# A transformer layer on one core: the transfer queue put into the program's order, with GpSimd's stores handed over some slots later

## The chip, the cores and the metric

The kernel runs on one core of a Trainium2 chip. The metric is the device time of one execution in microseconds (us). A core has a matrix engine (TensorE, PE in the profile; its weight loads are PEld), a vector engine (VectorE, DVE), an activation engine (ScalarE, ACT), GpSimd (POOL) and a queue that issues transfers (SyncE, SP; SPq marks its issues and waits). Each works through its own instructions in order and waits on semaphores for the others. Transfers move between HBM, which holds the inputs, the output and the kernel's scratch tensors, and on-chip memory.

## What is computed

```python
xn = layernorm(x)                                   # x: 2048 rows of 512
q, k, v = split(xn @ wqkv)                          # 32 heads of 16
p = softmax(q @ k.T * 16 ** -0.5)                   # per head, 2048 x 2048
a = concat_heads(p @ v) @ wo
m = gelu(xn @ w1 + b1) @ w2 + b2                    # hidden width 1792
out = x + a + m
```

Everything is in float32 at the interface. The kernel splits operands into a high and a low float16 part and adds the products of the parts.

## The kernel before

**Tiling.** Attention runs over 32 blocks, counted t = 0 to 31: 8 groups of 4 heads (`NG`) by 4 blocks of 512 queries (`NQB`). A block has 16 units. One call of `unit` (L582) issues 16 score products for unit u of the first pass (`s_half`, into `pS`; DVE takes the row maximum with L250), 16 transposed score products for unit u - 20 of the second pass (`e_half`, into `pT`; ACT exponentiates with L295), the products with v (`v_half`, into `pV`), and some dense products (`pD`) from a generator: the q and k projections first (`project`), then the two MLP products (`mlp`), then the output projection (`o_proj`).

**The hand-off of the maxima.** The second pass needs the negated row maxima of its block, which sit in two more rows of the q stack `qst`. When block t's first pass is over, `store` in `s_end` (L264) transposes the maxima on PE, DVE writes them to `mhl` (L271, L272), SP stores them to `m_d` (L275, two transfers), waits until they have landed, and loads them into `qst` (L280, four transfers). This stands in the program at the end of unit 16t + 16, and the first `pT` product of the block at the start of unit 16t + 20.

**What else goes through SP.** All transfers go through the one queue. Per block there is a chain for the softmax sums: `den_d<-osb` (L333), `dn<-den_d` (L360), a reciprocal on DVE (L336), `den_d<-dn` (L338), `rb<-den_d` (L342), three GpSimd operations (L346 to L348) and the store `ot_d<-ot` (L353). Head stacks `kst` and `qst` are loaded ahead (L392), MLP weights by `fetch_w1` (`wc<-w_d`, L540). In the projection phase GpSimd splits q and k results into `stg` (two buffers, L498 and L499), stored by L483 and L484, and weights into `wsp` (two buffers, L875 to L877), stored by L912 and L914. In the MLP's second product GpSimd adds to `xa`, stored by L995. At the end `oc<-ot_d` (L1006) and `ac<-acc_d` (L1011) load what the output projection needs; `out_dram<-ac` (L1016) stores the result.

**What sets the order.** `later(n, fn)` puts a piece of the program n slots later (a slot is one unit); `tick` (L226) runs what is due, and `pooled` steps for GpSimd are handed out on a budget of 2500 ns a slot. `flush` (L231), called after the projection phase and after the MLP, runs slots without units until no entry marked `True` (the third argument of `later`) is left. From L926 on, the engines in `ORDERED` keep the order in which the program was written. SP is not among them: a scheduler orders its transfers by its own estimates of when they are ready.

Of the kernel before, what the change touches and what calls it, by code (L numbers as in the profile page):

```python
# [25 lines left out]
NF = F // P  # L26
# [10 lines left out]
LFILL = (8, 16, 12, 12)  # L37
WARM = (14, 3, 2, 2)
FINE = "fine"
ORDERED = {mybir.EngineType.PE, mybir.EngineType.Activation, mybir.EngineType.DVE, mybir.EngineType.Pool}  # L40
GELU_C = 0.7978845608028654
GELU_A = 0.044715
MROW = 1024.0
# [4 lines left out]
def layer_kernel(ctx: ExitStack, tc: tile.TileContext, x, wqkv, wo, w1, b1, w2, b2, out):  # L48
# [110 lines left out]
    def given(engine, ns):  # L159
        backlog[engine] += ns  # L160
# [43 lines left out]
    def later(n, fn, local=False):  # L204
        queue.append((slot[0] + n, fn, local))
# [10 lines left out]
    def pooled(*todo):  # L216
        steps.extend(todo)
# [93 lines left out]
    def v_end(u):  # L311

        t, kt = divmod(u, 16)
        g, qb = divmod(t, NQB)
        for h in range(4):
            del ptiles[u, h]
        if kt < 15:
            return
        pv, k = pv_of.pop(t)
        osb = work.tile([P, QB], F32, name="osb", bufs=2)  # L320
        nc.scalar.activation(osb, pv, AF.Copy)
        given("act", 600)
        free_banks["S"].append(k)
        if t == NG * NQB - 1:
            later(1, lambda: last_one(osb))
            return

        dn = work.tile([64, 32], F32, name="dn", bufs=1)
        rb = work.tile([P, QB], F32, name="rb", bufs=1)

        def sums():
            for h in range(4):
                nc.sync.dma_start(den_d[t, 0, h:h + 1, :], osb[32 * h + DH:32 * h + DH + 1, :])  # L333

        def inverse():
            nc.vector.reciprocal(dn, dn)  # L336
            given("dve", 330)
            later(1, lambda: nc.sync.dma_start(den_d[t, 1].rearrange("h (c q) -> (h c) q", q=32), dn))  # L338

        def spread():  # L340
            for h in range(4):
                nc.sync.dma_start(rb[32 * h:32 * h + 32, :], den_d[t, 1, h:h + 1, :].to_broadcast([32, QB]))  # L342

        def store():
            ot = work.tile([P, 2, QB], F16, name="ot", bufs=2)
            pooled((1280, lambda: nc.gpsimd.tensor_tensor(osb, osb, rb, op=ALU.mult)),  # L346
                   (620, lambda: nc.gpsimd.tensor_scalar(ot[:, 0], osb, 1.0, 0.0, op0=ALU.mult, op1=ALU.add)),
                   (1160, lambda: nc.gpsimd.tensor_tensor(ot[:, 1], osb, ot[:, 0], op=ALU.subtract)),  # L348
                   (0, lambda: later(n, put)))

            def put():
                for h in range(4):
                    nc.sync.dma_start(ot_d[64 * g + DH * h:64 * g + DH * h + DH, :, qb * QB:(qb + 1) * QB],  # L353
                                      ot[32 * h:32 * h + DH])
                ready.add(t)


        n, far = (2, 3) if t < (NG - 1) * NQB else (1, 0)
        later(1, sums)
        later(2, lambda: nc.sync.dma_start(dn, den_d[t, 0].rearrange("h (c q) -> (h c) q", q=32)))  # L360
        later(2 + n + far, inverse)
        later(3 + 2 * n + far, spread)
        later(4 + 3 * n + far, store)
# [110 lines left out]
    def project(m, w, sb, wh, bank, early=False):  # L474

        prods = [lambda c=c, i=i, j=j: (wh[:, w, i, c, :], xt[:, j, c, sb * QB:(sb + 1) * QB])
                 for c in range(NC) for i, j in PAIRS]

        dst = qk_d[w, m * P:(m + 1) * P, :, sb * QB:(sb + 1) * QB]

        def finish(pj):
            def put():
                nc.sync.dma_start(dst[:, w:w + 2, :], stg)  # L483
                nc.sync.dma_start(dst[:, 2 - 2 * w, :], stg[:, 0])  # L484

            stg = ph.tile([P, 2, QB], F16, name="stg", bufs=2)
            given("act", 600)
            if early or (w == 1 and not m):
                nc.scalar.activation(stg[:, 0], pj, AF.Copy)
                nc.vector.tensor_tensor(stg[:, 1], pj, stg[:, 0], op=ALU.subtract)  # L490
            else:
                pf = ph.tile([P, QB], F32, name="pf", bufs=2)
                nc.scalar.activation(pf, pj, AF.Copy)
                if not m:
                    nc.scalar.activation(stg[:, 0], pj, AF.Copy)
                    nc.gpsimd.tensor_tensor(stg[:, 1], pf, stg[:, 0], op=ALU.subtract)
                else:
                    hi = lambda: nc.gpsimd.tensor_scalar(stg[:, 0], pf, 1.0, 0.0, op0=ALU.mult, op1=ALU.add)  # L498
                    lo = lambda: nc.gpsimd.tensor_tensor(stg[:, 1], pf, stg[:, 0], op=ALU.subtract)  # L499
                    later(1, lambda: pooled((620, hi), (1160, lo), (0, lambda: later(1, put, True))), True)  # L500
                    return

            put()

        return Group(prods, bank, finish)
# [31 lines left out]
    def fetch_w1(n):  # L537
        if n < NQB * NF:
            wcs[n] = feed[0].tile([P, 2, NC, P], F16, name="wc", bufs=3)
            nc.sync.dma_start(wcs[n], w1_d[n % NF])  # L540
# [89 lines left out]
    with ExitStack() as st1:  # L630
# [249 lines left out]
        def prepare():  # L880
            yield from ms
            am = work.tile([P, 10], F32, name="am_all")
            nc.vector.tensor_reduce(am[:, 0:7], amx[:, 0:7, :], axis=AX.X, op=ALU.max)
            nc.vector.tensor_reduce(am[:, 7:8], b1_s, axis=AX.X, op=ALU.max, apply_absolute_value=True)
            nc.vector.tensor_reduce(am[:, 8:9], amx[:, 7:14, :], axis=AX.XY, op=ALU.max)
            nc.vector.tensor_reduce(am[:, 9:10], amx[:, 14:16, :], axis=AX.XY, op=ALU.max)
            box = []
            yield
            yield from scales(am, 10, sbank, box)
            inv, fac = box  # L890
            fac1.append(fac)

            nc.vector.reduce_max(gs[:, 0:1], fac[:, 0:8], axis=AX.X)
            nc.vector.tensor_tensor(gs[:, 3:4], fac_v[0][:, 0:1], fac[:, 9:10], op=ALU.mult)
            yield
            nc.vector.reciprocal(gs[:, 1:2], gs[:, 0:1])
            nc.vector.tensor_tensor(gs[:, 2:3], gs[:, 0:1], fac[:, 8:9], op=ALU.mult)
            yield
            nc.vector.tensor_scalar_mul(gs[:, 1:2], gs[:, 1:2], 0.5)
            ended = [True]  # L900
            for n in range(16):
                v = fetch(16 + n)
                while not ended[0]:
                    yield
                ended[0] = False

                def then(wh=None, n=n):
                    ended[0] = True
                    if n < 7:
                        for a in range(2):  # L910
                            for l in range(2):
                                nc.sync.dma_start(w1_d[2 * n + a][:, l], wh[:, l, :, a * P:(a + 1) * P])  # L912
                    elif n < 14:
                        nc.sync.dma_start(w2_d[:, :, 2 * n - 14:2 * n - 12, :], wh)  # L914

                if n >= 14:
                    i = 2 * (n - 14)
                    split_steps(wo_s[:, 0, i:i + 2, :], wo_s[:, 1, i:i + 2, :], v, inv[:, 9:10], then)
                    continue
                wh = ph.tile([P, 2, 4, W] if n < 7 else [P, 2, 2, D], F16, name="wsp", bufs=2)  # L920
                k = n if n < 7 else 8
                split_steps(wh[:, 0], wh[:, 1], v, inv[:, k:k + 1], lambda wh=wh, then=then: then(wh))
            while not ended[0]:
                yield

        ctx.enter_context(tc.manual_schedule(engines=ORDERED))  # L926
        fil, pre, more = rest(), prepare(), True
# [7 lines left out]
    def mlp():  # L935
# [25 lines left out]
        for b in range(NQB):  # L961
            xb = xbs[b]
            g = m2.tile([P, 2, NF, QB], F16, name="g", bufs=1)
            for f in range(NF):
                fetch_w1(b * NF + f + 2)
                wc = wcs[b * NF + f]
                if b == 0 and f >= 3:
                    nc.sync.dma_start(w2_s[:, :, f - 3:NF if f == NF - 1 else f - 2, :],
# [13 lines left out]
            for q in range(4):  # L982
# [7 lines left out]
                def store(yp, xa=xa, t=t):  # L990
                    yt = m2.tile([P, D], F32, name="yt", bufs=2)
                    nc.scalar.activation(yt, yp, AF.Copy, scale=gs[:, 2:3])  # L992
                    given("act", 600)
                    add = lambda: nc.gpsimd.tensor_tensor(xa, xa, yt, op=ALU.add)  # L994
                    put = lambda: nc.sync.dma_start(acc_d[t * P:(t + 1) * P, :], xa)  # L995
                    later(1, lambda: pooled((1280, add), (0, lambda: later(1, put, True))), True)

                yield Group([lambda f=f, i=i, j=j, q=q, g=g: (g[:, i, f, q * P:(q + 1) * P], w2_s[:, j, f, :])
                             for f in range(NF) for i, j in PAIRS], dbank, store,
                            lambda n, b=b: (b, n // 3) in done, pace=SLOW if b < 2 else MEAN)  # L1000
# [125 lines left out]
```

## Time and profile before

| | |
|---|---|
| three runs | median 1655.86 us, 1652.38 to 1661.11 |
| the profiled execution | 1654.47 us |
| its span, first to last instruction | 1652.7 us |

The times of rows below are of that one execution and count from the start of its span. This part of its page gives the span in 40 slices of 41.3 us; each digit is a busy share in tenths, PEclk the granted clock of PE, DMA the share of the transfer engines:

```profile
PE   8998889988989999989999999899998999999998
DVE  8887769987988999989898999889898998999921
ACT  4317779987978998979898999888897898999993
POOL 3113577536762111767311167651115764111000
DMA  6466475341121111212111111221111110103122
```

PE, DVE and ACT are all near full from slice 8 on; GpSimd and the transfer engines are not. The projection phase fills slices 3 to 8, the MLP the slices to about 36, the output projection the rest.

### The profile page before, as it was taken

The numbers are of one execution on the slowest core, as the hardware profiler recorded it, in microseconds if no ns is written. First come the engines' busy times: TensorE is split into PE (matmuls) and PEld (weight loads), VectorE is DVE, ScalarE is ACT, GpSimd is POOL, SyncE is SP. The second block draws the span as 40 slices with busy tenths as digits, with TensorE's granted clock in tenths as the row PEclk, the third lists the DMA queues.
The fourth block names the chain that finished last, engine by engine and source line by source line (L and its number), as shares of the span: only waits on it lengthen the run. The fifth ranks groups of instructions, "written<-read, shape, count | busy, mean of one in ns | idle before, by whom it ended". The sixth has DMA issues, their size and how long they took to land.

```text
span 1652.7 us, 85954 instructions
## 1 busy us (share of the span) xinstructions
PE 1545.0 (93%) x38915; PEld 820.7 (50%) x38915; DVE 1427.7 (86%) x2420; ACT 1371.7 (83%) x2254; POOL 652.4 (39%) x678
## 2 busy tenths in 40 slices
PE   8998889988989999989999999899998999999998
PEld 3434445544544555545555555455554454554543
DVE  8887769987988999989898999889898998999921
ACT  4317779987978998979898999888897898999993
POOL 3113577536762111767311167651115764111000
PEclk9999999999999999999999999999999999999999
DMA  6466475341121111212111111221111110103122
GB/s 202 147 196 222 132 197 178 94 150 37 45 62 46 31 32 41 59 36 55 42 43 51 32 42 40 56 59 32 39 43 52 37 32 13 34 26 116 56 89 97
DMA packets 120248, 123.71 MB, mean 75 GB/s; under 512 B 38988, under 2 KB 90572, under 8 KB 119880
## 3 DMA queue, kind: packets, MB, share of 16 engines
q1 hardware_dynamic: 119880, 118.21, 24.4%
q8 instruction: 304, 4.98, 1.3%
q14 instruction: 64, 0.52, 0.1%
HBM read 80.61 MB, written 37.34 MB: 71 GB/s over the span
## 4 chain that ended last, share of the span: by engine, by line
PE 66%; DVE 20%; DMA 5%; issue 3%; POOL 3%; SPq 2%; ACT 1%; DVEq 0%; POOLq 0%
PE pV L169 20%; DVE mt L250 15%; PE pD L169 15%; PE pS L169 14%; PE pT L169 13%; DMA m_d<-mhl 3%; DVE hh L976 2%; DMA qst<-m_d 2%; PE pD L426 1%; PE pT L426 1%; DVE amx L648 1%; PE pT L519 1%; SPq L353 0%; POOL osb L346 0%; POOL ot L348 0%
## 5 line engine op out<-in xcount | busy, mean ns | idle before, releaser
L295 ACT ACTIVATE pe<-pT,sexp 128x512 f32<-128x512 f32 x2048 | 1270.1, 689 | 168.0 <-PE pT L169 110.8
L250 DVE TENSOR_REDUCE mt<-pS 128x1 f32<-128x512 f32 x2048 | 1290.9, 683 | 133.4 <-PE pS L169 112.4
L169 PE MATMUL pV<-pe,vv 64*32 64x512 f32 x8192 | 1098.4, 606 | 1.1 <-PE pS L169 0.7
L169 PE MATMUL pT<-qst,kst 64*32 64x512 f16 x8192 | 710.1, 385 | 67.4 <-DMA qst<-m_d 64.3
L169 PE MATMUL pS<-kst,qst 62*32 62x512 f16 x8192 | 657.6, 385 | 20.6 <-DVE mt L250 14.6
L169 PEld LDWEIGHTS <-kst 64*32 64x32 f16 x8192 | 291.8, 91 | 252.5 <-DMA qst<-m_d 79.6
L169 PEld LDWEIGHTS <-qst 62*32 62x32 f16 x8192 | 280.2, 93 | 263.5 <-issue 131.2
L169 PE MATMUL pD<-w_s,g 64*32 64x512 f16 x5376 | 370.9, 381 | 2.1 <-issue 2.1
L169 PE MATMUL pD<-xb,wc 64*32 64x512 f16 x5376 | 369.5, 384 | 0.6 <-issue 0.6
L169 PEld LDWEIGHTS pV<-pe,vv 64*32 64x32 f32 x8192 | 187.9, 106 | 102.5 <-PE pS L169 7.6
L169 PEld LDWEIGHTS <-wc 64*32 64x32 f16 x5376 | 123.5, 93 | 53.2 <-issue 4.3
L994 POOL TENSOR_TENSOR xa<-xa,yt 128x512 f32<-128x512 f32 x16 | 20.4, 1277 | 322.2 <-ACT yt L992 322.2
L169 PEld LDWEIGHTS <-g 64*32 64x32 f16 x5376 | 114.3, 92 | 46.8 <-issue 4.1
L956 POOL TENSOR_TENSOR t<-hh 128x512 f32<-128x512 f32 x56 | 58.2, 1039 | 196.0 <-DVE hh L976 182.1
L169 PE MATMUL pD<-xt,wqk_h 64*32 64x512 f16 x1920 | 131.6, 387 | 4.0 <-issue 4.0
L346 POOL TENSOR_TENSOR osb<-osb,rb 128x512 f32<-128x512 f32 x31 | 39.8, 1285 | 208.8 <-DMA rb<-den_d 118.2
L958 POOL TENSOR_TENSOR t<-t,hh 128x512 f32<-128x512 f32 x56 | 71.6, 1279 | 4.7
L951 POOL TENSOR_TENSOR t<-t,hh 128x512 f32<-128x512 f32 x56 | 71.5, 1276 | 4.7
L953 POOL TENSOR_TENSOR g<-t,g 128x512 f16<-128x512 f32 x56 | 65.1, 1162 | 4.7
L169 PEld LDWEIGHTS <-wqk_h 64*32 64x32 f16 x1920 | 44.8, 94 | 23.3 <-issue 8.9
L169 PE MATMUL pD<-wo_s,oc 64*32 64x512 f16 x768 | 50.1, 378 | 0.0
L950 POOL TENSOR_SCALAR t<-t,gs 128x512 f32<-128x512 f32 x56 | 38.8, 693 | 24.0 <-ACT t L945 24.0
(137 smaller groups left out, 824.9 us busy)
## 6 DMA issues: line engine op xcount, KB each, us to landing
wch<-in_B_w_dram SPq DMA_DIRECT2D x28, 512.0 KB
wc<-w_d SPq DMA_DIRECT2D x56, 256.0 KB
qk_d<-stg SPq DMA_DIRECT2D x32, 256.0 KB
rb<-den_d SPq DMA_DIRECT2D x124, 64.0 KB
kst<-qk_d SPq DMA_DIRECT2D x128, 48.0 KB
qst<-qk_d SPq DMA_DIRECT2D x128, 48.0 KB
xs<-in_A_x_dram SPq DMA_DIRECT2D x16, 256.0 KB
qk_d<-stg SPq DMA_DIRECT2D x32, 128.0 KB
```

Of the source, the lines that this page charges most:

```text
L169: p = nc.tensor.matmul(*args, **kw)
L250: nc.vector.reduce_max(mt_of[t][:, n, qt, kb:kb + 1], s, axis=AX.X)
L295: nc.scalar.activation(pe, st, AF.Exp, scale=sexp[:, g // 2:g // 2 + 1])
L346: pooled((1280, lambda: nc.gpsimd.tensor_tensor(osb, osb, rb, op=ALU.mult)), (620, lambda: nc.gpsimd.tensor_scalar(ot[:, 0], osb, 1.0, 0.0 ...
L426: nc.tensor.matmul(self.bank, lhs, rhs, start=start, stop=self.last and self.over())
L950: pooled((690, lambda: nc.gpsimd.tensor_scalar(t1, t1, 1.0, gs[:, 1:2], op0=ALU.add, op1=ALU.mult)), (1280, lambda: nc.gpsimd.tensor_tenso ...
L951: (1280, lambda: nc.gpsimd.tensor_tensor(t1, t1, hh, op=ALU.mult)),
L953: (1160, lambda: nc.gpsimd.tensor_tensor(g[:, 1, f, :], t1, g[:, 0, f, :], op=ALU.subtract)),
L956: pooled((1040, lambda: nc.gpsimd.tensor_tensor(t1, hh, hh, op=ALU.mult)), (620, lambda: nc.gpsimd.tensor_scalar(t1, t1, 1.0, 1.0 / GELU_A ...
L958: (1280, lambda: nc.gpsimd.tensor_tensor(t1, t1, hh, op=ALU.mult)),
L976: nc.vector.tensor_scalar(hh, hp, scale, bias, op0=ALU.mult, op1=ALU.add)
L994: add = lambda: nc.gpsimd.tensor_tensor(xa, xa, yt, op=ALU.add)
```

## The change

`ORDERED` gets SP, so that transfers stand in the order in which the program issues them. Stores of what GpSimd made are issued more slots later: `ot_d` 6 slots instead of 2 (still 1 in the last four blocks), `stg` 3 instead of 1, `wsp` 3 instead of at once, `xa` 4 instead of 1. `fetch_w1` inside the MLP is issued one slot later.

```diff
-ORDERED = {mybir.EngineType.PE, mybir.EngineType.Activation, mybir.EngineType.DVE, mybir.EngineType.Pool}
+ORDERED = {mybir.EngineType.SP, mybir.EngineType.PE, mybir.EngineType.Activation, mybir.EngineType.DVE, mybir.EngineType.Pool}
...
-                   (0, lambda: later(n, put)))
+                   (0, lambda: later(1 if n == 1 else 6, put)))
...
-                    later(1, lambda: pooled((620, hi), (1160, lo), (0, lambda: later(1, put, True))), True)
+                    later(1, lambda: pooled((620, hi), (1160, lo), (0, lambda: later(3, put, True))), True)
...
                     ended[0] = True
+                    later(3, lambda: put(wh, n), True)
+
+                def put(wh, n):
                     if n < 7:
...
-                fetch_w1(b * NF + f + 2)
+                later(1, lambda n=b * NF + f + 2: fetch_w1(n))
...
-                    later(1, lambda: pooled((1280, add), (0, lambda: later(1, put, True))), True)
+                    later(1, lambda: pooled((1280, add), (0, lambda: later(4, put, True))), True)
```

**SP around the hand-off of block 12** (the row `m_d<-mhl` is L275 of that block; `x4` counts equal transfers in a row). Before:

```order
L338 DMA den_d<-dn 64x32
L342 DMA rb<-den_d 32x512 x4
L540 DMA wc<-w_d 128x1024
L392 DMA kst_0_2_83<-qk_d 48x512 x2
L392 DMA kst_1_2_87<-qk_d 48x512 x2
L353 DMA ot_d<-ot 32x1x512 x4
L275 DMA m_d<-mhl 32x1x64 x2
L280 DMA qst_0_0_105<-m_d 2x4x128 x2
L280 DMA qst_1_0_109<-m_d 2x4x128 x2
```

With the change:

```order
L353 DMA ot_d<-ot 32x1x512 x4
L540 DMA wc<-w_d 128x1024 x2
L338 DMA den_d<-dn 64x32
L342 DMA rb<-den_d 32x512 x4
L540 DMA wc<-w_d 128x1024
L275 DMA m_d<-mhl 32x1x64 x2
L280 DMA qst_0_0_105<-m_d 2x4x128 x2
L280 DMA qst_1_0_109<-m_d 2x4x128 x2
L540 DMA wc<-w_d 128x1024
L333 DMA den_d<-osb 1x512 x4
```

The store of GpSimd's `ot` no longer stands between `rb` and the hand-off; the one that now stands further ahead is the previous block's. In all blocks but 30 and 31 what stands directly ahead of L275 is of this kind: loads, or stores whose data was made some slots ago.

**SP at the start of the ordered part** (the hand-off of block 0, and the loads of group 1's stacks, `kst_..._89` and following). Before, the 32 stack loads, of which the last two rows are shown, stand ahead of the hand-off:

```order
L392 DMA qst_0_3_108<-qk_d 48x512 x2
L484 DMA qk_d<-stg 128x512
L483 DMA qk_d<-stg 128x2x512
L392 DMA qst_1_3_112<-qk_d 48x512 x2
L275 DMA m_d<-mhl 32x1x64 x2
```

With the change they stand behind it:

```order
L275 DMA m_d<-mhl 32x1x64 x2
L280 DMA qst_0_0_97<-m_d 2x4x128 x2
L280 DMA qst_1_0_101<-m_d 2x4x128 x2
L392 DMA kst_0_0_89<-qk_d 48x512 x2
L392 DMA kst_1_0_93<-qk_d 48x512 x2
L392 DMA kst_0_1_90<-qk_d 48x512 x2
```

The first `stg` stores (L483, L484) now come after 20 of the 32 stack loads and two weight chunks.

**SP and DVE at the end.** On SP, ahead of the last hand-off (block 31), with the change:

```order
L353 DMA ot_d<-ot 32x1x512 x4
L1009 DMA oc<-ot_d 128x2x512 x4
L1014 DMA ac<-acc_d 128x512 x4
L1009 DMA oc<-ot_d 128x2x512 x3
L1009 DMA oc<-ot_d 64x2x512
L1014 DMA ac<-acc_d 128x512 x4
L275 DMA m_d<-mhl 32x1x64 x2
```

Before, six of these sixteen loads stood between `ot_d` and the hand-off, the other ten further ahead. On DVE the reciprocal of block 28 (L336) moves, because the second `flush` now runs more slots (L250 are the row maxima of blocks 29 and 30, `ac` is the output projection's). Before:

```order
L272 SCALAR_TENSOR_TENSOR mhl<-pS,mhl 64x64
L250 TENSOR_REDUCE mt<-pS 128x1 x28
L336 RECIPROCAL dn<-dn 64x32
L250 TENSOR_REDUCE mt<-pS 128x1 x32
L261 TENSOR_REDUCE mneg_118<-mt 128x16
```

With the change:

```order
L272 SCALAR_TENSOR_TENSOR mhl<-pS,mhl 64x64
L250 TENSOR_REDUCE mt<-pS 128x1 x20
L336 RECIPROCAL dn<-dn 64x32
L250 TENSOR_REDUCE mt<-pS 128x1 x40
L1018 SCALAR_TENSOR_TENSOR ac<-pD,gs,ac 128x512
```

It stands 8 reductions, two units, earlier; the output projection's products start three units earlier. Apart from this end, the order on PE, DVE, ACT and GpSimd is the same.

## The prediction

> **What bounds the kernel now.** I read the waits first, then the windows, then the timeline of one block.
>
> ```profile
> PE 1545.0 (93%) x38915; PEld 820.7 (50%) x38915; DVE 1427.7 (86%) x2420; ACT 1371.7 (83%) x2254; POOL 652.4 (39%) x678
> PE pT L169 <- DMA qst<-m_d: 64.3, 21, 6.1
> PE pS L169 <- DVE mt L250: 14.6, 46, 1.7
> DVE mt L250 <- PE pS L169: 112.4, 82, 6.4
> ACT pe L295 <- PE pT L169: 110.8, 89, 7.3
> ```
>
> PE is idle 1652.7 - 1545.0 = 107.7 us. In the waits (total, times, longest), 64.3 us of that is one thing: the first `pT` product of a block waits for the maxima loaded from `m_d`, 21 times. DVE and ACT wait for PE, not the reverse. So the hand-off through SP bounds those moments. Next, what SP itself waited for at the head of its queue:
>
> ```profile
> SPq L353 <- POOL ot L348: 176.8, 29, 10.9
> SPq L540 <- PE pT L169: 149.7, 36, 10.9
> ```
>
> Such waits hold up whatever stands behind them. Block 12 shows it in time order (start, us, engine; the bracket is idle time and its releaser):
>
> ```profile
> 703.89 0.22 DVE L272 SCALAR_TENSOR_TENSOR mhl<-pS,mhl 64x64 f16<-64x64 f32 x1
> 707.97 1.16 POOL L348 TENSOR_TENSOR ot<-osb,ot 128x512 f16<-128x512 f32 x1
> 709.15 2.49 SPq L353 DMA_DIRECT2D ot_d<-ot  x4
> 711.74 2.34 SPq L275 DMA_DIRECT2D m_d<-mhl  x2
> 715.30 1.16 SPq L280 DMA_DIRECT2D qst<-m_d  x4
> 717.17 0.64 PE L169 MATMUL pT<-qst,kst 64*32 64x512 f16 x8 [5.07 <-DMA qst<-m_d]
> ```
>
> `mhl` is ready at 704.11, but SP stands at L353 until GpSimd ends at 709.13, then issues four stores for 2.5 us. The hand-off starts 7.6 us late and PE waits 5.07 us. PE needed the rows at 717.17 - 5.07 = 712.10, 8.0 us after `mhl`. In block 13 no such store is in the way:
>
> ```profile
> 755.19 0.22 DVE L272 SCALAR_TENSOR_TENSOR mhl<-pS,mhl 64x64 f16<-64x64 f32 x1
> 755.43 1.22 SPq L275 DMA_DIRECT2D m_d<-mhl  x2
> 758.98 1.16 SPq L280 DMA_DIRECT2D qst<-m_d  x4
> ```
>
> The last issue ends at 760.14; with the 717.17 - 716.46 = 0.7 us that block 12 needed from there, the rows are in 5.4 us after `mhl`. That is 2.6 us inside the 8.0, and PE does not wait.
>
> The wait is not all. The windows (stretch, length, busy time by engine, PEclk, transfers) show what follows it:
>
> ```profile
> 173.60:1408.50 1234.90, 1152.22 (x31331) 633.74 (x31323) 1107.83 (x1833) 1082.08 (x1777) 576.31 (x573) 0.97 0.21 59
> 1408.50:1493.00 84.50, 84.50 (x2453) 47.73 (x2440) 82.93 (x137) 81.45 (x134) 16.69 (x15) 1.00 0.11 30
> 704.10:755.40 51.30, 45.51 (x1236) 24.44 (x1220) 44.19 (x75) 42.57 (x72) 31.65 (x34) 0.97 0.16 41
> 717.20:720.40 3.20, 3.20 (x56) 1.34 (x63) 0.87 (x2) 1.27 (x3) 0.00 (x0) 0.50 0.60 161
> 720.40:723.60 3.20, 3.20 (x104) 2.05 (x96) 2.85 (x5) 2.99 (x6) 0.00 (x0) 0.99 0.16 44
> ```
>
> After block 12's wait PE runs 3.2 us at half clock (0.50): DVE does 0.87 us of work there against 2.85 in the next 3.2 us. The first row spans 26 blocks that hold all 21 waits, the second two blocks with none: there DVE is busy 82.93 of 84.50 (98.1%) and bounds the pace.
>
> **The change part by part.**
>
> *The hand-off's queue.* With SP in program order and the stores handed over later, only things made some slots ago stand ahead of L275 in blocks 1 to 29. So the direct gain is the 64.3 us. On top comes the half clock. Two ends for the sum: 64.3 us if the ramp costs nothing, and, if the 26 blocks ran at the unhindered DVE share, 1234.9 - 1107.83 / 0.981 = 105.6 us. Block 12 by itself: 44.19 / 0.981 = 45.0 against 51.30 is 6.3 us for a wait of 5.07, a factor of 1.24, or 80 us on 64.3. Block 24 gives more:
>
> ```profile
> 1271.33 0.64 PE L169 MATMUL pT<-qst,kst 64*32 64x512 f16 x8 [4.57 <-DMA qst<-m_d]
> 1258.70:1310.80 52.10, 46.31 (x1228) 25.08 (x1213) 44.28 (x74) 42.61 (x71) 33.95 (x36) 0.93 0.15 44
> ```
>
> 44.28 / 0.981 = 45.1 against 52.10 is 7.0 us for 4.57, a factor of 1.53, or 98 us. I take **90 us**, between the two blocks' answers. What is late next is DVE's own work. Ahead of block 30's hand-off stands `out_dram<-ac`, which waits for an operation that is ahead of `mhl` on DVE too: 0.
>
> The half clock after a wait is what a page also speaks of. The Trainium skill, "TensorE: Matmul & The Clock Gate", Part 1, says that PE falls to half clock after an idle window of about 3.4 us and that the ramp is worth under 1% of a typical span for modelling. By that the ramp would be at most 16.5 us where I take 26, and the time 9 us higher. The trace does not agree on the window here:
>
> ```profile
> 897.71 0.48 PE L169 MATMUL pT<-qst,kst 64*32 64x512 f16 x8 [2.51 <-DMA qst<-m_d]
> 897.90:901.10 3.20, 3.20 (x56) 1.72 (x48) 1.27 (x2) 1.64 (x3) 0.00 (x0) 0.51 0.35 82
> ```
>
> A wait of 2.51 us is followed by half clock as well, so shorter waits pay too.
>
> *Later stores.* `ot_d` is read only by the output projection; `wsp` and `stg` hold two buffers each, so a later store may keep GpSimd from a buffer; `xa` likewise. GpSimd is busy 39%, which covers a few us. `fetch_w1` one slot later: the buffer is used two groups on, each group three units or more of about 3.0 us (1234.9 / 26 / 16), so 18 us less one slot; hidden, and 0 either way.
>
> *The start.* Block 0's hand-off now holds the queue until `mhl`, and 32 stack loads and the first `stg` stores come behind it.
>
> ```profile
> 116.27 0.22 DVE L272 SCALAR_TENSOR_TENSOR mhl<-pS,mhl 64x64 f16<-64x64 f32 x1
> 108.98 5.33 SPq L392 DMA_DIRECT2D qst<-qk_d  x9
> 115.82 0.38 SPq L483 DMA_DIRECT2D qk_d<-stg  x1
> 123.74 0.62 POOL L498 TENSOR_SCALAR stg<-pf 128x512 f16<-128x512 f32 x1 [5.37 <-ACT pf L493]
> 137.88 0.60 ACT L493 ACTIVATE pf<-pD 128x512 f32<-128x512 f32 x1
> ```
>
> From 116.5 on SP has the hand-off (about 3.5 us) and 22 issues at 5.33 / 9 = 0.6 us before the first store, so that is issued near 133 and not at 115.8, and lands near 135. The third `stg` operation of GpSimd (123.74) needs its buffer and starts some 12 us late; with the second one (1.2 us) it is through at about 137. ACT wants the `pf` buffer at 137.88. Bounds: nothing, or the whole 12 us if ACT waits; I take **2 us**, near the former, because 137 is just in time.
>
> *The end.* Block 28's reciprocal stands 8 reductions earlier:
>
> ```profile
> 1506.07 4.97 DVE L250 TENSOR_REDUCE mt<-pS 128x1 f32<-128x512 f32 x8 [0.34 <-PE pT L169]
> 1512.76 0.34 DVE L336 RECIPROCAL dn<-dn 64x32 f32<-64x32 f32 x1 [1.72 <-DMA dn<-den_d]
> 1505.75 1.11 SPq L333 DMA_DIRECT2D den_d<-osb  x4
> 1509.81 0.49 SPq L360 DMA_DIRECT2D dn<-den_d  x1
> ```
>
> DVE would come to it at about 1505.8 instead of 1511.0. Its input landed 2.95 us after an issue at 1509.81, which now follows L333 directly, at about 1507.5: ready at 1510.4. DVE waits 4.6 us, not 1.72: **+3 us** (0 to 5). Ahead of the last hand-off stand sixteen loads:
>
> ```profile
> 1568.12 2.48 SPq L353 DMA_DIRECT2D ot_d<-ot  x4
> 1572.16 1.93 SPq L1006 DMA_DIRECT2D oc<-ot_d  x3
> 1577.87 0.22 DVE L272 SCALAR_TENSOR_TENSOR mhl<-pS,mhl 64x64 f16<-64x64 f32 x1
> ```
>
> Sixteen at up to 0.64 from 1570.6 end at 1580.8, 2.7 us after `mhl` (1578.09): just about the 2.6 to spare; but they are 4 MB in flight, and the small stores may land behind them. Bounds 0 and 8 us; I take **+4**, the middle.
>
> *The sum.* 90 - 2 - 3 - 4 = 81 us off the profiled execution's own 1654.47 (span 1652.7 and 1.8 around it) is 1573.5. That execution is 1.4 below the median of the runs, so the median after should be **1575 us**. With all bounds against it the gain is 64.3 - 12 - 5 - 8 = 39 (1617), with all for it 105.6 (1550).
>
> **The rivals.**
>
> *The waits go, the rest does not.* DVE may eat the ramp term, being 90% busy over those 26 blocks already: the gain is 64.3 - 9, time 1600. For it: block 12's factor is only 1.24. Against: DVE did 0.87 us of work where it could do 2.85.
>
> *The skill's smaller ramp.* With at most 16.5 us for it, and the rows' costs, 64.3 + 16.5 - 9 = 72 and 1584. This lies in the forecast's own spread; I give it 0.15 of the 0.65 there, since block 24's factor of 1.53 speaks against it and block 12's does not.
>
> *Nothing gained.* Another wait takes the hand-off's place in each block, say `rb<-den_d` (L342), which now stands directly ahead of L275 and waits for DVE's reciprocal through L338. It would need to be over 2.6 us later than `mhl`. Against: it is issued in the slot before, from a reciprocal three slots before. The time stays at 1656.
>
> *Slower.* GpSimd's `wsp` buffers. Each of 14 splits (`wsp`) now gives its buffer back three slots (9 us) later, plus landing.
>
> ```profile
> 165.55 1.04 POOL L876 TENSOR_SCALAR wsp<-wch 128x1024 f16<-128x1024 f32 x1
> 174.06 1.04 POOL L876 TENSOR_SCALAR wsp<-wch 128x1024 f16<-128x1024 f32 x1
> ```
>
> Splits come every 8.5 us here, so a buffer is wanted again 17 us later and free 3.3 + 9 + 2 = 14.3 us later: covered. If the store is delayed so far that every split waits 8 us or more, GpSimd falls 14 x 8 = 112 us behind, ACT waits for its `pf` buffers, and 112 - 81 = 31 us is lost: 1687. It decides from 17 us on. Against: GpSimd is idle most of the time, and waits early in a chain widen the beat and end further waits.
>
> **How the numbers follow.** Forecast, 1558 to 1592: 0.65. Waits go but not the rest, 1592 to 1617: 0.17. More than forecast, under 1558: 0.08, half of it above 1550. Nothing gained: 0.05. Slower: 0.05. The range 1550 to 1617 is the sum with all bounds one way and the other and holds about 0.86. A measurement of this kernel can tell about 0.5% from no change; so faster 0.90, same 0.05, slower 0.05.
>
> **What would show it.** In the waits of the changed kernel `PE pT <- DMA qst<-m_d` should be gone in blocks 1 to 29, a few us in all; PEclk 1.00 in the windows of those blocks; DVE at 97% or more there; SP waiting for DVE `mhl` at L275 most of all. GpSimd `stg` should wait about 12 us near 124. DVE should wait 4 to 5 us at the reciprocal of block 28. It is wrong if L275 is issued over 2.6 us after `mhl` in the middle blocks, if ACT waits for GpSimd's `pf` before 300 us, or if the blocks stay longer than DVE's work with no wait of PE left.

## The result, and the profile after

| | before | changed |
|---|---|---|
| median | 1654.12 us | 1567.61 us |
| lowest to highest | 1652.20 to 1661.11 | 1564.89 to 1572.93 |
| ratio | | 0.947 (95% interval 0.9435 to 0.9508) |
| the profiled execution, its span | 1654.47, 1652.7 | 1564.89, 1563.1 |

The profiled executions differ by 89.6 us, the medians by 86.5; 81 were predicted. The same lines of the changed kernel's page, the totals and the slices:

```profile
PE 1513.9 (97%) x38915; PEld 810.6 (52%) x38915; DVE 1424.6 (91%) x2420; ACT 1369.7 (88%) x2254; POOL 654.0 (42%) x678
...
PE   8998989999999999999999999999999999999988
...
DVE  8899878899999999999999999999999999998801
```

The work is the same (the instruction counts are equal), but PE idles 49.2 us instead of 107.7. Its waits, of PE and at the head of SP's queue:

```profile
PE pS L169 <- DVE mt L250: 15.9, 47, 3.3
PE pT L169 <- DMA qst<-m_d: 8.9, 3, 4.5
...
SPq L275 <- DVE mt L250: 157.2, 28, 8.4
...
SPq L644 <- POOL wsp L877: 27.7, 9, 5.5
SPq L353 <- POOL ot L348: 11.3, 3, 5.0
```

The wait for the maxima fell from 64.3 us to 8.9. SP now stands at L275 before the maxima are there, 157.2 us in all, and at GpSimd's `ot` 11.3 us, not 176.8. Block 12 in order of time:

```profile
658.92 0.22 DVE L272 SCALAR_TENSOR_TENSOR mhl<-pS,mhl 64x64 f16<-64x64 f32 x1
659.16 1.20 SPq L275 DMA_DIRECT2D m_d<-mhl  x2
...
661.58 1.16 SPq L280 DMA_DIRECT2D qst<-m_d  x4
...
666.72 0.39 PE L169 MATMUL pT<-qst,kst 64*32 64x512 f16 x2
```

The store is issued at once after `mhl`, and PE's first product has no bracket: no idle time ahead of it. The windows of the 26 blocks from block 1, of blocks 28 and 29, and of block 12:

```profile
169.10:1307.40 1138.30, 1119.03 (x31327) 624.63 (x31319) 1104.72 (x1833) 1079.55 (x1777) 577.91 (x573) 1.00 0.24 66
1307.40:1391.80 84.40, 84.40 (x2450) 48.01 (x2440) 82.91 (x137) 81.33 (x134) 16.77 (x15) 1.00 0.11 33
659.10:703.50 44.40, 43.68 (x1236) 24.09 (x1220) 44.09 (x75) 42.56 (x72) 31.82 (x34) 1.00 0.28 73
```

The 26 blocks take 1138.3 us instead of 1234.9, 96.6 less, and DVE is busy 97.0% of them. Block 12 takes 44.4 instead of 51.3.

To see where kernels differ, I cut each profiled span at the end of `mhl` (L272) in block 5 and in block 27:

| profiled execution | to block 5 | 5 to 27 | 27 to the end | span |
|---|---|---|---|---|
| before | 377.3 | 1031.2 | 244.2 | 1652.7 |
| changed | 358.7 | 948.7 | 255.7 | 1563.1 |
| changed, a second time | 361.4 | 948.5 | 254.9 | 1564.8 |
| the program's order only | 355.7 | 950.1 | 250.1 | 1555.9 |
| the same, a second time | 357.5 | 950.1 | 249.5 | 1557.1 |
| the later delays only | 381.9 | 1026.3 | 250.5 | 1658.7 |
| changed, `stg` and `wsp` as before | 356.2 | 949.4 | 256.1 | 1561.7 |
| changed, `wsp` as before | 360.6 | 950.0 | 255.8 | 1566.4 |
| changed, `ot_d` and `fetch_w1` as before | 362.2 | 949.3 | 254.7 | 1566.2 |
| changed, last `xa` store early | 368.2 | 950.8 | 250.9 | 1569.9 |
| changed, third output block's loads late | 360.5 | 948.0 | 248.2 | 1556.7 |
| order only, third output block's loads late | 356.2 | 949.8 | 243.7 | 1549.7 |

The middle is the same to 3 us in every kernel of the table with SP in program order. The start and the end are not, and there lies what the prediction missed.

### The profile page after: what moved, and what is told of

Same layout as the page of the kernel before. It is cut to its first block, busy times and chain, and to the rows that moved or that the text cites. A ratio compares the mean times of both kernels' runs of the same rounds, so it can differ in the third digit from the quotient of the medians.

```text
span 1563.1 us, 85813 instructions
## 1 busy us (share of the span) xinstructions
PE 1513.9 (97%) x38915; PEld 810.6 (52%) x38915; DVE 1424.6 (91%) x2420; ACT 1369.7 (88%) x2254; POOL 654.0 (42%) x678
## 3 DMA queue, kind: packets, MB, share of 16 engines
q8 instruction: 304, 4.98, 1.4%
## 4 chain that ended last, share of the span: by engine, by line
PE 73%; DVE 17%; DMA 4%; issue 3%; SPq 1%; POOL 1%; ACT 1%; DVEq 0%; POOLq 0%; ACTq 0%
PE pV L169 22%; PE pD L169 17%; PE pS L169 15%; PE pT L169 15%; DVE mt L250 12%; DVE hh L979 2%; DMA m_d<-mhl 1%; PE pD L426 1%; PE pT L426 1%; DMA oc<-ot_d 1%; PE pT L519 1%; SPq L392 1%; DVE amx L648 0%; POOL osb L346 0%; PE pV L519 0%
## 5 line engine op out<-in xcount | busy, mean ns | idle before, releaser
L250 DVE TENSOR_REDUCE mt<-pS 128x1 f32<-128x512 f32 x2048 | 1288.3, 683 | 38.4 <-PE pS L169 22.8
L169 PE MATMUL pV<-pe,vv 64*32 64x512 f32 x8192 | 1082.6, 598 | 2.0 <-issue 0.9
L169 PE MATMUL pS<-kst,qst 62*32 62x512 f16 x8192 | 637.7, 379 | 19.9 <-DVE mt L250 15.9
L169 PE MATMUL pD<-w_s,g 64*32 64x512 f16 x5376 | 365.4, 377 | 0.4 <-issue 0.4
L169 PE MATMUL pD<-xb,wc 64*32 64x512 f16 x5376 | 360.8, 377 | 0.0
L169 PEld LDWEIGHTS pV<-pe,vv 64*32 64x32 f32 x8192 | 181.9, 105 | 101.6 <-PE pS L169 7.6
L169 PEld LDWEIGHTS <-wc 64*32 64x32 f16 x5376 | 120.1, 91 | 52.7 <-issue 1.9
L979 DVE TENSOR_SCALAR hh<-pD,fac,b_s 128x512 f32<-128x512 f32 x56 | 45.3, 809 | 1.2
```

Source lines behind the costliest of these rows:

```text
L169: p = nc.tensor.matmul(*args, **kw)
L250: nc.vector.reduce_max(mt_of[t][:, n, qt, kb:kb + 1], s, axis=AX.X)
L979: nc.vector.tensor_scalar(hh, hp, scale, bias, op0=ALU.mult, op1=ALU.add)
```

## The experiments

### Which part brings the gain

**The order alone:** the kernel before with this one line.

```diff
-ORDERED = {mybir.EngineType.PE, mybir.EngineType.Activation, mybir.EngineType.DVE, mybir.EngineType.Pool}
+ORDERED = {mybir.EngineType.SP, mybir.EngineType.PE, mybir.EngineType.Activation, mybir.EngineType.DVE, mybir.EngineType.Pool}
```

> The kernel before with one edit: SP keeps the program's order; every delay is the old one. Theory A (the order alone brings the gain): in program order the store of ot stands behind the hand-off in every block, whatever its delay, so the 64.3 us of waits and their half clock go: 1565 to 1585 us, PE waiting for qst at most 25 us in all. Theory B (the delays are needed, since in program order SP stands at stores of GpSimd's results with all else behind them): SP waits for POOL over 150 us in all, at xa, wsp, stg and ot, and hand-offs or weight chunks come late: 1600 us or more.

Measured: 1557.81 us (1554.63 to 1559.53), ratio 0.942 (0.9388 to 0.9445). That is theory A, and 9.8 us less than with the whole change. In its waits, SP stands at GpSimd's stores for some tens of us, but only one hand-off is late:

```profile
PE pT L169 <- DMA qst<-m_d: 4.0, 1, 4.0
...
SPq L995 <- POOL xa L994: 36.0, 8, 9.6
SPq L353 <- POOL ot L348: 17.9, 8, 6.0
```

**The delays alone:** the changed kernel without SP in `ORDERED`.

```diff
-ORDERED = {mybir.EngineType.SP, mybir.EngineType.PE, mybir.EngineType.Activation, mybir.EngineType.DVE, mybir.EngineType.Pool}
+ORDERED = {mybir.EngineType.PE, mybir.EngineType.Activation, mybir.EngineType.DVE, mybir.EngineType.Pool}
```

> The changed kernel without SP in the program's order; the later stores and the later weight fetch stay. Theory A: the same rows stand directly ahead of the hand-offs as before the change, the store of ot in about two blocks of three, so nothing is gained: 1645 to 1660 us, and 55 to 70 us of PE waiting for qst. Theory B (the delays are the part that counts): 1600 us or less.

Measured: 1662.56 us (1658.10 to 1669.29), ratio 1.005 (1.0032 to 1.0075), so a little slower than before, and its waits are like those of before:

```profile
PE pT L169 <- DMA qst<-m_d: 70.2, 22, 11.1
...
SPq L353 <- POOL ot L348: 175.2, 29, 10.9
```

A later place in the program does not move `ot_d` behind the hand-off as long as a scheduler orders the queue. The order does it, with the old delays as with the later ones.

**Both again,** each with runs of the kernel before beside it, since the delays seemed to cost time:

> The changed kernel once more, as the measure for the runs beside it. Both theories: 1563 to 1573 us. Theory E (the five later hand-overs cost time, since the program's order alone took 1557.8 us): it is 7 to 13 us slower than that. Theory F (the two differ by chance): within 4 us of it.

> The kernel before with SP in program order and every old delay, once more and in more rounds, as the measure for the runs beside it. Theory E (the later hand-overs cost time): 1555 to 1561 us. Theory F (its lead over the changed kernel was chance): 1563 to 1570 us.

Measured: the changed kernel 1568.91 us (ratio 0.948, 0.9453 to 0.9504), the order alone 1556.30 (0.940, 0.9381 to 0.9422). The intervals are apart, and theory E holds: the five delays cost 10 to 13 us.

### What a wait of PE costs

**24 late hand-offs:** in the changed kernel, blocks 4 to 27 hand over two slots later.

```diff
-        later(1, store)
+        later(3 if 4 <= t < 28 else 1, store)
```

> The changed kernel with the hand-offs of blocks 4 to 27 put two slots later, so that each should make PE wait: two slots of 2.8 us less the slack of 2.6, about 3.0 us in each of 24 blocks, 72 us in all. Theory A (a wait costs itself and the half clock behind it, 1.24 to 1.53 per us of wait): 1567.6 plus 89 to 110, 1657 to 1678 us, granted clock of the 24 blocks 0.95 to 0.98. Theory C (only the wait is lost): 1640 us. Theory D (DVE makes up for part of the wait out of its own slack): below 1630 us.

**The same, with the wait filled** by twelve products ahead of the block's first `pT` product, in the same bank, which that product overwrites:

```diff
+FILL = 12
...
         k0 = (kt % 4) * P
+        if kt == 0 and n == 1 and 4 <= t < 28:
+            for _ in range(FILL):
+                tiled(None, st, kst[g % 2][p][0][r, k0:k0 + P], kst[g % 2][p][0][r, :], True, True)
```

> As the kernel with 24 late hand-offs, and PE is given twelve more products of 64 rows by 512 columns (in four column tiles each) ahead of the first product that waits; their result is overwritten by it. They need only data that is there, so PE works through most of the wait. Theory A (the excess is the half clock that follows idle time): the waits stay as long counted from mhl, but the clock stays at 1.00, and the time falls to 1640 us (1567.6 + 72), 17 to 38 us below the kernel without them. Theory C (the excess, if there is any, has another cause, such as the refilling of the chain of buffers): within 8 us of the kernel without them.

Measured: 1652.70 us (1643.27 to 1659.33) and 1631.52 (1629.88 to 1634.29). The waits were shorter than expected. In the profiled execution of the first kernel the waits for `qst` are 63.1 us, of which 5.6 belong to block 2 and 3.5 to block 31, so 54 us are those made late, and not 72: the 2.6 us of slack came from a block whose stores took 2.3 us to land, and most take 1.2. The medians of this kernel and the changed one are 85 us apart, below theory A's time. Like must be set against like, and the profiled execution was one of the faster ones: its span of 1643.1 us is 80 above the changed kernel's 1563.1, so its 54 us of waits cost a factor of 1.48. Giving PE something to do in the wait took back 21 us of the median, though no transfer came sooner: the last issue into `qst` ended 4.10 us after `mhl` in the mean of the 24 blocks, and 4.12 with the filling. Windows of the first kernel, each 3.41 us long, show why:

```profile
560.10:563.51 3.41, 2.33 (x60) 0.82 (x44) 3.07 (x5) 2.29 (x4) 0.00 (x0) 1.00 0.05 7
563.51:566.92 3.41, 1.50 (x41) 0.83 (x46) 0.69 (x1) 0.99 (x2) 0.00 (x0) 1.00 0.01 2
973.10:976.51 3.41, 0.75 (x28) 0.08 (x14) 1.41 (x3) 0.76 (x2) 3.16 (x4) 1.00 0.02 4
976.51:979.93 3.42, 3.42 (x56) 1.85 (x64) 1.22 (x2) 1.58 (x3) 0.10 (x1) 0.50 0.29 77
```

A wait of 2.66 us lies inside the third window and leaves PE 0.75 us of work there; the fourth runs at half clock, and DVE does 1.22 us of work in it. The wait in the first two is longer, 2.99 us, but lies across the edge, 1.08 and 1.91 us idle, and nothing follows. In the kernel with the filled wait, whose lines are numbered one higher here, one place in order of time and the window of the 24 blocks:

```profile
962.86 2.54 PE L170 MATMUL pT<-kst 64*32 64x512 f16 x44
...
965.84 0.43 PE L170 MATMUL pT<-qst,kst 64*32 64x512 f16 x8 [0.44 <-DMA qst<-m_d]
```

```profile
319.70:1431.80 1112.10, 1095.28 (x30224) 606.56 (x30216) 1033.78 (x1707) 1004.24 (x1650) 484.56 (x494) 1.00 0.17 48
```

Its clock is 1.00; over the same stretch of time the kernel without the filling has 0.98. The time also goes with the clock from one execution to the next. The clock that an execution lost is (1 - its mean clock) times its span. Over the ten executions with empty waits it goes from 27.9 to 48.1 us, and the time follows it with 0.77 us per us lost; drawn out to no loss, that line ends at 1622.5 us. The four with filled waits, by their own line, end at 1623.8. Both lines are drawn beyond few points; that they meet fits a filling that changed the clock and little else. Theory A holds for the 21 us. What remains, 64 us over the changed kernel, is not the waits alone: the twelve products take PE 2.76 us in each block, 66 us in all, where the waits that they fill were 2.35 us in the mean, and 6 us of waits are left in those blocks. So the clock may be worth more than 21 us here; how much of the remainder is the filling's own length, and how much a chain of buffers that has to fill again, was not separated.

### What the delays cost

**`stg` and `wsp` as before,** and `wsp` alone as before (the first of these edits without the second):

```diff
-                    later(3, lambda: put(wh, n), True)
+                    put(wh, n)
...
-                    later(1, lambda: pooled((620, hi), (1160, lo), (0, lambda: later(3, put, True))), True)
+                    later(1, lambda: pooled((620, hi), (1160, lo), (0, lambda: later(1, put, True))), True)
```

> The changed kernel with the old hand-over of both stg and wsp. Theory M (these two delays cost the start 3 to 5 us, since block 5's maxima are ready at 358.7 to 361.4 us with them and at 355.7 without any delay): 1563 to 1566 us, maxima of block 5 ready at 355 to 357 us. Theory N (the starts differ by what PE loses in issue from one execution to the next, not by these delays): 1566 to 1571 us.

> The changed kernel, but the stores of wsp are handed over at once and not three slots later. Theory I (three slots later they stand ahead of block 2's hand-off, where SP waits for GpSimd, as SP's 5.94 and 3.53 us there say): block 2's wait of 4.5 us and the half clock behind it go, 4 to 7 us less than the changed kernel. Theory J (at once they make SP wait for GpSimd in other places, with loads and hand-offs behind them): no gain, or up to 6 us slower, with a wait of PE for qst somewhere in blocks 1 to 5.

Measured: 1564.88 us (ratio 0.946, 0.9435 to 0.9477) and 1566.98 (0.947, 0.9441 to 0.9495). With both undone, block 5's maxima are ready at 356.2 us, as theory M said, and its time lies where M put it, though the interval of its ratio overlaps the changed kernel's. With `wsp` alone undone, block 2's wait is gone as theory I said, but not the time: the start ends at 360.6. Nor is it J, as no hand-off is late. PE loses 9.6 us there in waits for which the profile shows no releaser (2.1 in the changed kernel, 4.4 with both undone). What they are is open.

Block 2 of the changed kernel shows what the delays do. SP's rows (L915 stores `wsp`, L912 before the change):

```profile
206.61 5.94 SPq L915 DMA_DIRECT2D w_d<-wsp  x8
212.65 0.50 SPq L338 DMA_DIRECT2D den_d<-dn  x1
216.59 0.37 SPq L644 DMA_DIRECT2D wch<-in_B_w_dram  x1
217.02 0.46 SPq L483 DMA_DIRECT2D qk_d<-stg  x1
217.53 0.46 SPq L484 DMA_DIRECT2D qk_d<-stg  x1
218.09 2.01 SPq L342 DMA_DIRECT2D rb<-den_d  x4
220.14 3.53 SPq L915 DMA_DIRECT2D w_d<-wsp  x4
223.77 1.22 SPq L275 DMA_DIRECT2D m_d<-mhl  x2
```

and GpSimd's, with the end of the block's wait on PE:

```profile
213.29 1.05 POOL L876 TENSOR_SCALAR wsp<-wch 128x1024 f16<-128x1024 f32 x1 [4.17 <-DMA w_d<-wsp]
214.43 2.14 POOL L877 TENSOR_TENSOR wsp<-wch,wsp 128x1024 f16<-128x1024 f32 x1
...
229.03 0.58 PE L169 MATMUL pT<-qst,kst 64*32 64x512 f16 x8 [4.50 <-DMA qst<-m_d]
```

GpSimd waits 4.17 us for the late store of a `wsp` buffer. So it ends L877 only at 216.57, and SP, whose load of `wch` wants the buffer that L877 reads, stands at L644 from 213.2 to 216.59. The hand-off, ready at 215.43, goes out behind all of these at 223.77, 8.3 us late.

**`ot_d` and `fetch_w1` as before:**

```diff
-                   (0, lambda: later(1 if n == 1 else 6, put)))
+                   (0, lambda: later(n, put)))
...
-                later(1, lambda n=b * NF + f + 2: fetch_w1(n))
+                fetch_w1(b * NF + f + 2)
```

> The changed kernel with the old hand-over of ot_d and the weight fetch at once. Theory O (both edits are hidden, since ot's store stands behind the hand-off in program order either way, and the weights are wanted two groups later): within 4 us of the changed kernel, 1565 to 1571 us. Theory P (the ot delay is what keeps SP from waiting at L353 with the next block's sums behind it): 1575 us or more.

Measured: 1568.34 us (ratio 0.948, 0.9455 to 0.9495), between the changed kernel's two medians. Theory O.

### The end

**The last `xa` store early:**

```diff
-                    later(1, lambda: pooled((1280, add), (0, lambda: later(4, put, True))), True)
+                    later(1, lambda: pooled((1280, add), (0, lambda: later(1 if t == NT - 1 else 4, put, True))), True)
```

> The changed kernel, but the very last store of xa is handed over 1 slot later and not 4, so the second flush has as few slots as before and block 28's reciprocal stands again behind 28 reductions, not 20. Theory G (DVE's wait of 3.9 us at that reciprocal, PE's gap of 3.3 us and the half-clock window behind it are a loss): the gap near 1409 us goes, and the time falls by 4 to 7 us against the changed kernel. Theory H (the end is bound by what comes behind, so the loss there is made up): within 2 us.

Measured: 1565.00 us (0.946, 0.9437 to 0.9488), 3.9 less than the changed kernel beside it, which the runs alone do not tell from no change. The end of the profiled execution does: 250.9 us from block 27, against 254.7 to 256.1 in the five executions with that store late. In the changed kernel:

```profile
1408.46 0.34 DVE L336 RECIPROCAL dn<-dn 64x32 f32<-64x32 f32 x1 [3.93 <-DMA dn<-den_d]
...
1409.41 0.40 PE L169 MATMUL pS<-kst,qst 62*32 62x512 f16 x4 [3.27 <-DVE mt L250]
```

With the early store the same two brackets are 1.90 and 1.92. I take theory G for the mechanism, with 4 to 5 us.

**The third output block's loads behind the last hand-off:**

```diff
-            if n < NQB:
+            if n < NQB and (n != 2 or pos[0] > NU + 1):
...
-                    yield from o_proj(qb, *blocks[qb][0])
+                    for f in o_proj(qb, *blocks[qb][0]):
+                        yield f
+                        if qb == 1:
+                            fetch_o()
```

> The changed kernel, but the third output block's eight loads are issued behind block 31's hand-off and not ahead of it. Theory K (these loads hold the hand-off up, 4.0 us in the queue and more in the landing): PE's gap of 4.2 us at 1493 goes with the two half-clock windows behind it, 4 to 7 us less than the changed kernel. Theory L (the loads are needed by then, so the output projection comes late by as much): within 2 us, with a wait for oc or ac in the last 70 us.

Measured: 1560.78 us (0.943, 0.9410 to 0.9458), 8.1 less than the changed kernel beside it, 7 of it at the end. In the changed kernel:

```profile
1479.48 2.84 SPq L1009 DMA_DIRECT2D oc<-ot_d  x4
1482.37 2.50 SPq L1014 DMA_DIRECT2D ac<-acc_d  x4
1485.41 1.61 SPq L275 DMA_DIRECT2D m_d<-mhl  x2
1491.32 1.18 SPq L280 DMA_DIRECT2D qst<-m_d  x4
```

`mhl` is ready at 1481.40, and L275 goes out at 1485.41, behind the loads. Then L280 waits till 1491.32, 4.3 us, for its two small stores to land. With eight of the loads put behind the hand-off:

```profile
1481.92 1.24 SPq L275 DMA_DIRECT2D m_d<-mhl  x2
1486.12 1.18 SPq L280 DMA_DIRECT2D qst<-m_d  x4
```

The queue is free when `mhl` is ready, and PE no longer waits; the landing still takes 3.0 us after the last issue (the last section comes back to it).

**The order alone with this edit:**

> The program's order alone, and the third output block's eight loads behind block 31's hand-off. Theory K: its gap of 4.0 us at 1487 and the half-clock window at 1488 go, 4 to 7 us less than the program's order alone, 1551 to 1554 us, below both kernels of the case. Theory L (what was saved in the changed kernel's longer end is not there to be saved here): within 2 us of it.

Measured: 1551.48 us (1547.95 to 1554.18), ratio 0.937 (0.9349 to 0.9396). It has the lowest median of all: 16 us below the changed kernel and 4.8 below the order alone. The intervals of the last two overlap, but the end of the profiled executions tells them apart (249.5 to 243.7 us). Theory K again.

## Why the prediction was right, and where not

- **The direct wait, 64.3 us: right.** 8.9 us are left, nearly all at blocks 2 and 31.
- **The half clock, 26 us on top: right in kind, a little small.** The 26 blocks gained 96.6 us. 4.8 us of waits are left in that stretch, so 59.5 of the gain is waits, and 37 is on top where 26 were taken. The clock's record has 21 half-clock windows of 3.41 us in that stretch before and one after: 34 us if all the lost half counted. The filled waits show that such a term is real. The rivals that gave the ramp nothing (1600) or at most 16.5 us (1584) fell. The upper end, 105.6, took DVE at 98.1%, and it came to 97.0%. That DVE bounds the pace was read from two blocks in which PE was busy for all of the 84.50 us too, so that reading was not shown.
- **"Only things made some slots ago stand ahead of L275 in blocks 1 to 29": wrong for block 2.** The step that failed is `wsp`, costed at nothing because a buffer would be free 14.3 us after a split and wanted after 17. The 17 came from one pair of splits. Later splits of the same execution are closer:

```profile
209.26 1.04 POOL L876 TENSOR_SCALAR wsp<-wch 128x1024 f16<-128x1024 f32 x1
215.55 1.04 POOL L876 TENSOR_SCALAR wsp<-wch 128x1024 f16<-128x1024 f32 x1
221.84 1.04 POOL L876 TENSOR_SCALAR wsp<-wch 128x1024 f16<-128x1024 f32 x1
```

These come every 6.3 us, so a buffer is wanted again after 12.6, before it is free. In the changed kernel GpSimd waited for stores of `wsp` seven times, 17.7 us in all, where the profile before lists no such wait. This sets off the wait of SP at L644, which the prediction did not follow: a load that wants a buffer holds the queue too. The slower rival had this mechanism; it cost 4.5 us of PE and the half clock behind it, not 112.
- **The start, +2 us: the mechanism came as said, the sum did not.** GpSimd's third `stg` operation came at 136.14 instead of 123.74, and ACT then waited 1.73 us for its buffer:

```profile
136.14 0.62 POOL L498 TENSOR_SCALAR stg<-pf 128x512 f16<-128x512 f32 x1 [17.80 <-DMA qk_d<-stg]
...
138.03 0.60 ACT L493 ACTIVATE pf<-pD 128x512 f32<-128x512 f32 x1 [1.73 <-POOL stg L499]
```

Over the five profiled executions with `stg` and `wsp` both late and no hand-off put late, block 5's maxima came at 362 us in the mean, against 356.4 over the four in program order without either delay: about 6 us for the two delays at the start, 4 without the slowest of the five. How much of that is this place, for which the sum had 2, and how much is `wsp`, was not separated.
- **The reciprocal of block 28, +3 us: right place, too small.** DVE waited 3.93 us (4.6 were said), but the window behind PE's gap ran at half clock, which the term left out; the end shows 4 to 5 us.
- **The sixteen loads, +4 us: right place, too small.** Moving eight of them behind the hand-off took 7 us off the end. In the changed kernel the hand-off stood 4.0 us in the queue and landed 3.1 us later than most, and two half-clock windows followed PE's wait.
- **The signs that it named.** The clock of 1.00, DVE's 97% and the late `stg` near 124 us came. One sign of being wrong came as well: ACT waited for GpSimd's `pf` before 300 us, 4.3 us in three places, where before it was 2.0 in one. L275 was issued at once after `mhl` in all blocks but 2 and 31. SP's longest wait was not at L275 but at L338 for the reciprocal, 189.6 us in all.
- **The sum.** 90 - 9 = 81 was predicted and 89.6 measured, because terms of both signs were too small: +96.6 in the 26 blocks and 4.5 more up to block 1, less 11.5 behind block 27. The gains were 13 us more than the sum had and the losses at the end 4.5, so that it came so near is in part luck. Among the five executions with both stores late, block 5 came between 358.7 and 368.2 us, so a part of the start is chance.
- **What the prediction did not ask:** whether each part of the change is needed. It costed the delays at 3 us, the reciprocal's, and took them for a part of what the order needs. The order alone gives all of the gain, and the delays take 10 to 13 us of it back: 4 to 6 at the start (`stg` and `wsp`), about 5 at the end (the last `xa` store), nothing for `ot_d` and `fetch_w1`.

## What to carry to other kernels

In a queue that works strictly in order, look for the small transfer that an engine waits for, and at what stands ahead of it; moving that took one line here and was worth more than the wait itself. Try each part of such a change alone: here one line made the gain, and the four kinds of precaution beside it made it smaller. A store handed over later holds its buffer longer, and the wait comes back at the next user of the buffer, or at a load behind it in the same queue.

## What the hardware showed

- **The clock is decided on a fixed grid.** In each trace the half-clock stretches begin on one grid of 3413 ns. In every trace of this case, each full-clock window of the grid with over 2.0 us without a product was followed by one at half clock, and none with under 1.0 us; between these both were seen. So a wait of 1.9 us may cost clock, and the one of 2.99 us above did not, by where it falls, and the kernel with 24 short waits spread over 16 us in ten executions, where the same kernel with them filled spread over 4.4 in four. The Trainium skill, "TensorE: Matmul & The Clock Gate", Part 1, states a free-running window of 3413 ns, which these traces show. It also says that the clock falls after at least one idle window; here some 60% of a window was enough. Its figure of under 1% of a typical span is said of one warm-up, and the prediction took it for all the waits together; the execution before, with 21 waits, lost 2.4% of its clock.
- **Small stores landed late in two ways.** In the changed kernel L280 is issued 1.2 us after L275's last issue in 25 of the 32 blocks, which is the landing of two small stores. Each store lands in sixteen parts. In two blocks all parts came late, behind large loads: the wait is 4.3 us in block 31, behind sixteen loads, and 4.1 in block 21, behind stack loads, `xb` and `xa`. In blocks 10, 13 and 18 it is 2.5 to 2.9 us with no large load ahead; there one or two parts of the two stores come late, and a packet of another queue runs at that time, the one that the page lists as

```profile
q8 instruction: 304, 4.98, 1.4%
```

These are 304 packets, 4.98 MB in all, of 16 KB each. The twelve traces with SP in program order have 308 hand-offs whose two stores were issued without a pause. In 61 of them such a packet began less than 1.0 us after the last issue and ended more than 0.1 us after it. All 61 landed more than 1.4 us after the last issue, 58 of them 1.0 to 1.6 us after the packet's end. Of the other 247, 14 landed late, five of them in block 21. That fits a part of a store standing behind such a packet; no run changes the packets, so the cause is not shown. The 3.0 us of block 31 with eight loads ahead is such a case, and so is block 13 before the change, 2.3 us, from which the 2.6 us to spare in the prediction were counted.
